# Attention, top-1 experts and a gated product on one core: the first pair's swapped k on TensorE, the last gate's row table inside the written order, own buffers for the last g tile

## The chip, the cores and the metric

The kernel runs on one core of one Trainium2 chip. The metric is the device time of one execution in microseconds (us); lower is better. Before the change the median of three runs is 1043.4 us (1043.09 to 1043.55).

## The reference

Three stages follow each other, all in fp32. The matrix products of the kernel work on pairs of fp32r tiles, a high and a low part of each number, with three products for one.

```python
# attention: 4 batches, 8 heads, 576 positions, 64 wide
scores = q @ k.T / sqrt(64)
scores = where(scores >= rowmax - tau, scores, -1e9)
x = softmax(scores) @ v                       # 2304 tokens x 512
# experts: 8, 1024 wide, the best one for each token
logits = x @ w_gate
g = softmax(logits)[best]
x = g * (relu(x @ w1[best]) @ w2[best])
# gated product, 1536 wide
out = ((x @ w_a) * (x @ w_b)) @ w_out
```

## The kernel before

**Attention** (class `Attention`, lines 257 to 1230). Sixteen pairs of heads are numbered 0 to 15, four for a batch. For a pair, k and q are loaded, split into high and low (`kh`, `kl`, `qh`, `ql`, lines 405 to 437), transposed by TensorE (`qk`, line 460 for four blocks of 128 positions, lines 484 and 485 for the tail of 64 positions) and copied out of PSUM (`qe`). A score product needs k twice, once with its high and low halves swapped between the partitions; the swapped copy `kT[:, 1]` is made by DMA from `kT[:, 0]` (`swap`, line 466; units `sk0` and `sk2`). The nine score tiles of a pair (`s`, line 677; J is the one of the two tails) are followed by the row maximum (`m`, line 690), the threshold (`th`, line 694), the exponential (`e`, line 698) and the masked product (`p`, line 710). The probabilities are transposed (line 785), split (lines 738 to 750) and multiplied with v (line 861, stacked halves `tk` by DMA, line 806), and the result is multiplied with W (line 887), which holds an identity and the gate's columns. The work of several pairs overlaps.

After each batch a **gate** (lines 950 to 1068) takes the expert of each token, counts with small products how many tokens of each expert came before (`tr`), forms the slot of each token (`slot`, lines 1016 to 1027), adds the batch's counts to the running first rows (`base`, line 1037), scales the tokens (`xg0` to `xg3`, `xh`) and scatters them by GpSimd to their expert's rows in DRAM (`sc0` to `sc4`, line 44).

While the last pair runs, a **lead** item already computes 256 rows of one expert from the first three batches (lines 523 to 650): weights are loaded one by one in three raw buffers (`l_wl`, lines 568 and 570), split (`l_wh`, `l_wd`, lines 583 to 589; w1 on ScalarE and VectorE, w2 on GpSimd), and used by eight first products (`l_ap`, line 601; relu `l_ah`, `l_ad`, lines 606 and 610) and eight second ones (`l_b`, line 625).

The order of all this is written out by hand: `ORDER` is a list of some 2750 names, and `emit` calls the units in that order. Each engine executes its own instructions in turn; SyncE's queue does so with the DMAs that it issues.

**Experts** (class `Experts`). `order` (line 1299) sorts the experts by their number of rows and writes a table of the expert, its first rows and count, `ti`. SyncE reads it (line 1605), loads the first expert's rows (`xr`, line 1510), which also need every scatter to have landed, and then the raw weights (line 1440). The rows are transposed (`px`, line 1530), copied and split (lines 1532 and 1533), the weights are split (lines 1446 and 1447), and products follow (lines 1555 and 1576). `order` is no part of the written order; the framework places it between.

**Gated product** (`gated`, line 1711). Seven groups of the 1536 columns go over five chunks of 512 tokens, the last of 256. `front` makes a and b (line 1743), a copy (line 1750), their product (line 1752) and its high and low part `gh`, `gl` (lines 1754 and 1756), in rings of three buffers. `back` makes the output product (line 1769) and adds it to `acc` (line 1774); it is issued one chunk behind `front`. In the last group each finished tile of 128 tokens is scattered to the output (line 44).

```python
    gh, gl = [ap.tile([P, 512], F32R, tag=f"g{r}", bufs=3, name=f"g{r}_{g}_{c0}_{j}") for r in range(2)]
    nc.scalar.copy(gh[:, 0:n], gt[:, 0:n])
    low = nc.vector if (g, c0) == (ng - 1, chunks[-1][0]) else nc.gpsimd
```

## Time and profile before

| | |
|---|---|
| median of three runs | 1043.4 us |
| the profiled execution | 1042.98 us |
| its span, first to last instruction | 1041.3 us |
| TensorE busy in the span | 1003.0 us (96%) |
| VectorE | 713.3 us (68%) |
| ScalarE | 541.7 us (52%) |
| GpSimd | 562.6 us (54%) |

The profile is of one execution. PE is TensorE's products, PEld its weight loads, DVE VectorE, ACT ScalarE, POOL GpSimd, SP SyncE; a q behind an engine's name is its queue, which also issues DMAs. L785 is line 785 of the kernel. A row of the order in time gives the start and the length of a group of like instructions in us, and in brackets how long the engine was idle before it and what ended that. Products are pipelined and their ends are modelled, so that the length of a group is a little more than its number times the distance of two. PEclk is the granted clock of TensorE as a share of full speed (2.4 GHz; half is 1.2 GHz).

### The profile page before, as it was taken

What the parts mean: (1) busy time and instruction counts of PE and PEld (TensorE: products, weight loads), DVE (VectorE), ACT (ScalarE), POOL (GpSimd) and SP (SyncE); (2) the same over time, 40 slices, a digit from 0 to 9 for tenths busy, and PEclk for the clock granted to TensorE, in tenths of its full rate; (3) what the DMA queues carried; (4) which work ended last, traced back from release to release, by engine and by line L of the source; (5) the groups of instructions that cost most, each with busy time, mean ns of one, the idle gap of its engine ahead of it and who ended that gap; (6) DMA issues with size and microseconds to landing.
All of it is one profiled execution on the core that took longest, in us unless ns stands there. A gap on an engine that the chain in (4) does not pass through costs nothing.

```text
span 1041.3 us, 18663 instructions
## 1 busy us (share of the span) xinstructions
PE 1003.0 (96%) x6392; PEld 910.2 (87%) x6392; DVE 713.3 (68%) x1454; ACT 541.7 (52%) x1118; POOL 562.6 (54%) x522
## 2 busy tenths in 40 slices
PE   5899999999999899999999999999999999999996
PEld 4799999999999889999999988888888888888885
DVE  6999999999997545555599488843953945834222
ACT  4999999999996354455565344321322312321110
POOL 4888898998987521111234267633633734623334
PEclk9999999999999989999999999999999999999999
DMA  6778645445344486556666123510210310300012
GB/s 164 216 208 226 183 122 133 110 130 132 104 119 148 163 261 210 168 172 180 191 197 210 34 81 74 68 41 1 63 59 1 81 41 21 82 1 1 31 51 101
DMA packets 111777, 119.20 MB, mean 114 GB/s; under 512 B 20064, under 2 KB 82528, under 8 KB 111680
## 3 DMA queue, kind: packets, MB, share of 16 engines
q1 hardware_dynamic: 107248, 106.93, 37.0%
q0 software_dynamic: 3840, 10.50, 2.7%
q8 instruction: 51, 0.84, 0.3%
q10 hardware_dynamic: 592, 0.56, 0.2%
q14 instruction: 46, 0.38, 0.1%
HBM read 77.57 MB, written 20.98 MB: 95 GB/s over the span
## 4 chain that ended last, share of the span: by engine, by line
PE 52%; issue 5%; POOL 3%; DVE 3%; ACT 1%; POOLq 0%; DVEq 0%; ACTq 0%
PE pg L1743 22%; PE po L1769 10%; PE py_i L1576 9%; PE ph_i L1555 9%; POOL out L44 1%; PE px_i L1530 1%; POOL w L1478 1%; POOL t L1477 1%; DVE acc L1774 1%; DVE a L1469 1%; DVE w L1447 1%; POOL g L1756 0%; DVE t L1473 0%; DVE u L1470 0%; ACT w L1476 0%
## 5 line engine op out<-in xcount | busy, mean ns | idle before, releaser
L1743 PE MATMUL pg<-y,w 128*128 128x512 f32 (+1 forms) x1440 | 301.9, 368 | 0.0
L1743 PEld LDWEIGHTS pg<-y,w 128*128 128x128 f32 x1440 | 251.6, 189 | 45.3
L1756 POOL TENSOR_TENSOR g<-gg,g 128x512 fp32r<-128x512 f32 (+1 forms) x58 | 76.2, 1314 | 151.0 <-ACT g L1754 150.9
L1769 PE MATMUL po<-w,g 128*128 128x512 f32 x648 | 153.3, 390 | 0.6 <-DVE acc L1774 0.6
L1769 PEld LDWEIGHTS po<-w,g 128*128 128x128 f32 x648 | 120.9, 188 | 26.2 <-issue 0.8
L1447 POOL TENSOR_TENSOR w<-raw,w 128x512 fp32r<-128x512 f32 x33 | 45.3, 1373 | 160.5 <-ACT w L1446 154.3
L750 POOL TENSOR_TENSOR pt<-st,pt 128x512 fp32r<-128x512 f32 x93 | 119.8, 1295 | 10.1 <-ACT pt L740 7.2
L1754 ACT CAST g<-gg 128x512 fp32r<-128x512 f32 (+1 forms) x60 | 34.7, 578 | 170.1 <-PE po L1769 97.3
L1555 PE MATMUL ph_i<-xt_i,w 128*128 128x256 f32 (+4 forms) x768 | 118.9, 302 | 4.3 <-DVE w L1447 2.4
L1752 DVE TENSOR_TENSOR gg<-ga,pg 128x512 f32<-128x512 f32 (+1 forms) x60 | 37.7, 629 | 122.0 <-PE pg L1743 122.0
L1576 PE MATMUL py_i<-h_i,w 128*128 128x256 f32 (+4 forms) x768 | 114.0, 297 | 0.3 <-PEq L1670 0.3
L1555 PEld LDWEIGHTS ph_i<-xt_i,w 128*128 128x128 f32 x768 | 106.9, 192 | 6.0 <-DVE w L1447 3.1
L1576 PEld LDWEIGHTS py_i<-h_i,w 128*128 128x128 f32 x768 | 106.5, 192 | 0.7 <-ACT w L1446 0.6
L861 PE MATMUL pv<-pt,sv 128*128 128x288 f32 x512 | 103.3, 317 | 0.2 <-ACT o L866 0.2
L1774 DVE TENSOR_TENSOR acc<-acc,po 128x512 f32<-128x512 f32 x108 | 72.7, 683 | 34.6 <-PE po L1769 34.6
L785 PE MATMUL tp<-idf,P 128*128 128x128 f32 x504 | 89.9, 274 | 2.2 <-DVE P L710 1.3
L1477 POOL TENSOR_TENSOR t<-t,w 128x512 f32<-128x512 f32 x36 | 53.2, 1478 | 64.0 <-ACT w L1476 47.7
L1446 ACT CAST w<-raw 128x512 fp32r<-128x512 f32 x128 | 75.7, 618 | 15.0 <-PE py_i L1576 5.9
L1447 DVE TENSOR_TENSOR w<-raw,w 128x512 fp32r<-128x512 f32 x95 | 68.3, 730 | 11.0 <-ACT w L1446 9.0
L861 PEld LDWEIGHTS pv<-pt,sv 128*128 128x128 f32 x512 | 75.0, 190 | 0.8 <-ACT o L866 0.6
L1560 DVE SCALAR_TENSOR_TENSOR h_i<-ph_i,h_i 128x256 fp32r<-128x256 f32 (+4 forms) x64 | 28.8, 451 | 62.5 <-ACT h_i L1559 62.5
L1559 ACT ACTIVATE h_i<-ph_i 128x256 fp32r<-128x256 f32 (+4 forms) x64 | 26.1, 407 | 83.5 <-PE ph_i L1555 62.7
(249 smaller groups left out, 1920.0 us busy)
## 6 DMA issues: line engine op xcount, KB each, us to landing
raw<-in_moe_w SPq DMA_DIRECT2D x128, 256.0 KB
xs<-zero SPq DMA_DIRECT2D x32, 320.0 KB
tk<-half SPq DMA_DIRECT2D x64, 144.0 KB
raw<-in_moe_w_a SPq DMA_DIRECT2D x12, 512.0 KB
raw<-in_moe_w_b SPq DMA_DIRECT2D x12, 512.0 KB
raw<-in_moe_w_out SPq DMA_DIRECT2D x12, 512.0 KB
kT<-kT SPq DMA_DIRECT2D x32, 160.0 KB
kT<-kT SPq DMA_DIRECT2D x30, 144.0 KB
```

Of the source, the lines that this page charges most:

```text
L750: nc.gpsimd.tensor_sub(lo, st, fr(hi))
L785: nc.tensor.transpose(st["ps"][:, 128 * j:128 * j + 128], parts(j), idf)
L861: nc.tensor.matmul(R["v", n][:, 0:HALF], lhs, z, start=(c == 0 and r == 0), stop=(c == 4))
L1446: nc.scalar.copy(hi_t, raw)
L1447: engine.tensor_sub(lo_t, raw, fr(hi_t))
L1477: g.tensor_sub(t, t, fr(hi))
L1555: nc.tensor.matmul(ps[:, 0:n], w[a][:, k, :], xt[b][k][:, 0:n], start=(s_ == 0), stop=(s_ == len(steps) - 1))
L1576: nc.tensor.matmul(st["y"][d][:, 0:n], w[a][:, 0, d * P:d * P + P], h[b][:, 0:n], start=(f == 0 and d % each == 0 and (a, b) == (0, 0)), s ...
L1743: mm = nc.tensor.matmul(ps[:, 0:n], w[g][j][m][a][:, k, :], self.y[b][:, k, c0:c0 + n], start=(s_ == 0), stop=(s_ == len(steps) - 1))
L1756: last = low.tensor_sub(gl[:, 0:n], gt[:, 0:n], fr(gh)[:, 0:n])
L1769: nc.tensor.matmul(ps, res[j][a][:, t * P:t * P + P], w[g][j][2][b][:, 0, :], start=(s_ == 0), stop=(s_ == len(steps) - 1))
L1774: nc.vector.tensor_tensor(acc[:, tt, :], acc[:, tt, :], ps, op=ALU.add)
```

## The change

- Pair 0: GpSimd splits the tails of k and q (units `kH`, `qH`, `kL`, `qL`), a second copy of k's high part is laid behind the low part (`k3` on ScalarE, `K3` for the tail on GpSimd), and TensorE transposes low and high in that order (`sk0`, `sk2`, and a third block of the tail). ScalarE and VectorE copy the results to `kT[:, 1]`. The four swap DMAs of this pair are gone. The tails' loads are split in two DMAs of 64 rows each, k's on SyncE's and q's on ScalarE's queue; tau goes to SyncE's queue. In the order the constants (`c:r`, `c:m`) come first, the tail's transposes before all others, and the zero fills of `qj` and `z` go from VectorE to GpSimd.
- Last gate: `order` is gone. Its instructions are in the last gate's `base`, in two new units `places` and `table`, and three of them in the lead's selection; most operands lie in the PSUM bank of the gate's counts. The integer table comes straight from a sum, no longer from a copy. In the new order the five last scatters stand in a row behind `table`.
- Gated product: in the last chunk of the last group the second `gh`, `gl` get the buffers of two tiles of the weight splits (`mag`, `t`), and the last tile's output product and sum are done in two halves of 256 columns.
- `ORDER` is new throughout.

```diff
 ORDER = """
-qh:0 qH:0 kh:0 kl:0 qk:0:k2 qk:0:k0 kH:0 qe:0:k2 kL:0 ql:0 qL:0 c:z qk:0:t qe:0:k0 qe:0:kt qk:0:q0 qk:0:q1 c:t qe:0:q1
-qe:0:q0 qe:0:sk0 qe:0:t qe:0:sk2 s:0 qh:1 c:r ql:1 kh:1 kl:1 z:10 z:17 vh:0 vl:0 lv:1 vh:1 vl:1 c:w s:1 qk:1:t qe:1:t
+c:r c:m kh:0 qh:0 k3:0 kl:0 kH:0 qH:0 kL:0 qL:0 K3:0 qk:0:t qk:0:k0 qe:0:ks qe:0:k0 qk:0:k2 c:z qk:0:sk0 qk:0:sk2 ql:0
+c:t qe:0:k2 qk:0:q0 qk:0:q1 qe:0:sk2 qe:0:q1 qe:0:t qe:0:sk0 qe:0:kt lk:2 kh:1 kl:1 vh:0 vl:0 qh:1 ql:1 qe:0:q0 s:0
...
+s:1 m:0 m:1 e:0 th:1 p:0 e:1 qk:1:t qe:1:t qk:1:k0 qk:1:q0 qe:1:q0 qe:1:k0 qe:1:kt s:2 p:1 s:3 m:2 m:3 th:3 e:2 p:2
...
+l_wh:4:0 l_wd:4:0 l_wl:4:1 l_b:0 x1s:15 x1t:15 lt:gate:15 tl:gate:15 L:gate:15 top:gate:15 shift:gate:15 ex:gate:15
+g:gate:15 l_ap:2 l_ah:2 l_ad:2 l_b:1 tr:gate:15 l_hint slot:gate:15 base:gate:15 l_wh:4:1 l_wd:4:1 l_wl:5:0 l_wh:5:0
+xg0:gate:15 l_wd:5:0 l_wl:5:1 l_wh:5:1 l_wd:5:1 xg3:gate:15 l_ap:3 l_ah:3 l_ad:3 places:gate:15 l_b:2 xg1:gate:15
+xg2:gate:15 l_ap:4 l_ah:4 xh:gate:15 table:gate:15 l_ad:4 l_b:3 l_ap:5 sc0:gate:15 sc1:gate:15 sc2:gate:15 sc3:gate:15
+sc4:gate:15 gate:15 l_wl:6:0 l_wh:6:0 l_wd:6:0 l_wl:6:1 l_wh:6:1 l_wd:6:1 l_wl:7:0 l_wh:7:0 l_ah:5 l_wd:7:0 l_wl:7:1
...
         for n in "kq":
-            nc.sync.dma_start(self.state[0]["raw_" + n][:, 8, :], two[n][:, 512:576].rearrange("a s d -> a s d"))
+            for a in range(2):
+                (nc.sync if n == "k" else nc.scalar).dma_start(self.state[0]["raw_" + n][64 * a:64 * a + 64, 8, :], two[n][a, 512:576])
...
             for z in self.qj:
-                nc.vector.memset(fr(z), 0.0)
-            nc.vector.memset(self.z, 0.0)
+                nc.gpsimd.memset(fr(z), 0.0)
+            nc.gpsimd.memset(self.z, 0.0)
...
+        def again(z):
+            def run():
+                o, x = s["sk"][:, z, 2, :], s["raw_k"][:, z]
+                if z == tail:
+                    nc.gpsimd.tensor_scalar(o, x, 1.0, 1.0, op0=ALU.mult, op1=ALU.mult)
+                else:
+                    nc.scalar.copy(o, x)
+            return run
...
+        def again(n):
+            def front():
+                if "S" not in ps:
+                    ps["S"] = self.psS.tile([P, 2, 512], F32R, tag="S", name="again")
+                for j in range(4):
+                    nc.tensor.transpose(ps["S"][:, n, P * j:P * j + P], kb(4 * n + j, 1), idr)
+
+            def back():
+                (nc.vector.tensor_copy if n else nc.scalar.copy)(tile("kT")[:, 1, 640 * n:640 * n + 512], flat(ps["S"])[:, n])
+            return front, back
...
             pre = G["pre"]
-            if b == self.B - 2:
+            if last:
+                counts[:] = cnt, key, G2 = bank(112, E), bank(120, E), bank(128, E * E)
+                v.tensor_tensor(cnt, pre[:, 5], r["rest"], op=ALU.add)
+                v.scalar_tensor_tensor(key, cnt, float(E), r["io"], op0=ALU.mult, op1=ALU.subtract)
+                same = new("key", [P, E])
+                v.tensor_copy(same, key)
+                v.tensor_copy(r["src"][:, 2, :], cnt)
+                v.tensor_tensor(grid(G2), key.unsqueeze(1).to_broadcast([P, E, E]), same.unsqueeze(2).to_broadcast([P, E, E]), op=ALU.is_gt)
+            elif b == self.B - 2:
...
+        def table():
+            big = bank(256, 4 * E * E).rearrange("p (z a b) -> p z a b", z=4, a=E)
+            shape = [P, 4, E, E]
+            v.tensor_tensor(big, grid(bank(192, E * E)).unsqueeze(1).to_broadcast(shape), r["src"].unsqueeze(2).to_broadcast(shape), op=ALU.mult)
+            with nc.allow_low_precision(reason="one whole number and zeros"):
+                v.tensor_reduce(r["ti"], big, axis=AX.X, op=ALU.add)
+            v.tensor_reduce(r["T"], big, axis=AX.X, op=ALU.add)
+            v.tensor_copy(r["st"], bank(48, E))
+            self.psT.done(G["pr"])
...
-                    gh, gl = [ap.tile([P, 512], F32R, tag=f"g{r}", bufs=3, name=f"g{r}_{g}_{c0}_{j}") for r in range(2)]
+                    end = (g, c0) == (ng - 1, chunks[-1][0])
+                    if end and j:
+                        gh, gl = [self.cv.tile([P, 512], F32R, tag=z, name=f"g_{z}") for z in ("mag", "t")]
+                    else:
+                        gh, gl = [ap.tile([P, 512], F32R, tag=f"g{r}", bufs=3, name=f"g{r}_{g}_{c0}_{j}") for r in range(2)]
...
+                    wide = DM // 2 if (g, tt) == (ng - 1, ntile - 1) else DM
+                    for z in range(0, DM, wide):
+                        z = slice(z, z + wide)
```

## Rows read from the trace of the kernel before

**Rows 1.** Busy time by stage: length, then engines (instructions), PEclk, DMA share, GB/s.
```profile
0.00:16.00 16.00, 5.13 (x26) 4.41 (x27) 10.16 (x41) 4.83 (x10) 7.36 (x25) 1.00 0.64 161
...
100.00:200.00 100.00, 98.17 (x785) 92.74 (x785) 92.34 (x239) 94.68 (x203) 89.85 (x92) 1.00 0.55 149
...
337.00:360.00 23.00, 21.00 (x175) 20.32 (x174) 14.78 (x49) 6.94 (x15) 14.25 (x14) 1.00 0.40 135
360.00:374.00 14.00, 9.45 (x40) 8.91 (x41) 5.91 (x11) 6.83 (x14) 4.85 (x5) 0.63 0.72 241
374.00:1017.00 643.00, 639.84 (x3581) 566.28 (x3580) 381.35 (x604) 223.94 (x449) 247.91 (x190) 1.00 0.32 91
```

**Rows 2.** Waits of TensorE, 60 to 345 us: us in all, times, longest.
```profile
PE pv L861 <- DMA tk<-half: 1.3, 2, 0.6
```

**Rows 3.** Instructions in order of time, start of the kernel.
```profile
4.81 1.26 PE L460 MATMUL tq<-idr,sk 128*128 128x128 f32 x8 [4.81 <-DVE sk L428]
...
6.86 0.24 ACT L419 CAST sq<-raw_q 128x64 fp32r<-128x64 f32 x1 [1.90 <-DMA raw_q<-in_q]
7.01 0.58 ACT L476 CAST kT<-tq 128x512 fp32r<-128x512 f32 x1
...
14.48 1.81 PE L677 MATMUL S_J<-kT,qj 128*128 128x288 f32 x6 [3.99 <-DMA kT<-kT]
```

**Rows 4.** GpSimd's groups up to 345 us: count, busy us, mean ns of one.
```profile
L827 POOL TENSOR_TENSOR pt<-js,pt 128x256 fp32r<-128x256 f32 x32 | 23.8, 748 | 7.9 <-ACT pt L826 7.8
...
L589 POOL TENSOR_TENSOR l_w<-l_raw,l_w 128x512 fp32r<-128x512 f32 x5 | 7.0, 1402 | 0.3
L717 POOL TENSOR_SCALAR J<-J 128x64 f32<-128x64 f32 x16 | 4.0, 250 | 0.3 <-DVE J L710 0.2
...
L585 POOL TENSOR_SCALAR l_w<-l_raw 128x512 fp32r<-128x512 f32 x5 | 3.1, 621 | 4.2 <-DMA l_raw<-in_moe_w 4.2
```

**Rows 5.** VectorE in order of time, 343 to 358 us.
```profile
343.64 0.22 DVE L1027 TENSOR_SCALAR si<-slot,role 128x1 int32<-128x1 f32 x1
...
349.32 0.42 DVE L610 SCALAR_TENSOR_TENSOR l_h<-l_ph,l_h 128x256 fp32r<-128x256 f32 x1 [2.20 <-ACT l_h L606]
...
352.81 0.69 DVE L589 TENSOR_TENSOR l_w<-l_raw,l_w 128x512 fp32r<-128x512 f32 x1 [2.09 <-ACT l_w L583]
...
355.40 0.80 DVE L1327 TENSOR_TENSOR o_big<-o_M,src 128x256 f32<-128x256 f32 x1
...
356.69 0.70 DVE L1331 CAST o_ti<-o_T 128x32 int32<-128x32 f32 x1
```

**Rows 6.** The other engines in order of time, 351 to 373 us.
```profile
351.82 0.99 POOL L44 DMA_INDIRECT xs<-xg,si  x1 [0.30 <-issue]
...
354.70 1.69 PE L601 MATMUL l_ph<-l_xT,l_w 128*128 128x256 f32 x12 [1.52 <-DVE l_h L610]
...
358.53 0.37 SPq L1510 DMA_DIRECT2D xr_i<-xs  x1
...
362.49 2.58 PE L1530 MATMUL px_i<-idf,xr_i 128*128 128x128 f32 x12 [2.56 <-DMA xr_i<-xs]
...
366.83 6.23 PE L1555 MATMUL ph_i<-xt_i,w 128*128 128x352 f32 x24 [1.76 <-ACT w L1446]
```

**Rows 7.** Instructions in order of time, the tail.
```profile
1018.25 5.92 PE L1743 MATMUL pg<-y,w 128*128 128x256 f32 x48
...
1024.00 8.35 PE L1769 MATMUL po<-w,g 128*128 128x512 f32 x36
...
1028.76 0.41 ACT L1754 CAST g<-gg 128x256 fp32r<-128x256 f32 x1 [5.57 <-PE po L1769]
1029.20 0.42 DVE L1756 TENSOR_TENSOR g<-gg,g 128x256 fp32r<-128x256 f32 x1 [0.21 <-ACT g L1754]
...
1032.16 1.28 DVE L1774 TENSOR_TENSOR acc<-acc,po 128x512 f32<-128x512 f32 x2 [1.80 <-PE po L1769]
...
1034.41 0.98 POOL L44 DMA_INDIRECT out<-acc,i_idc  x1 [0.30 <-issue]
```

More of the change, by code (lines that the diff above doesn't have):

```diff
@@ L342, in rest, with more @@
                 )
+        def more():
+            i2, ji = tiles["i2"], tiles["ji"]
+            routing.update(routing.pop("late")())
             nc.vector.tensor_copy(self.II, i2.unsqueeze(1).to_broadcast([P, 2, D]))
@@ L365, in wide @@
             nc.vector.tensor_copy(self.WT[:, :, W:WT], self.W2[:, 4:8, D:W])
-        self.setup = {"t": scales, "z": zeros, "r": rest, "w": wide}
+        self.setup = {"t": scales, "z": zeros, "r": rest, "w": wide, "m": more}
     def load(self, i, names):
@@ L426, in run @@
                 t = s["s" + n][:, z]
-                g = nc.vector if n != "v" and (i, n) in self.FIRST else nc.gpsimd
+                g = nc.vector if n != "v" and (i, n) in self.FIRST and not (i == 0 and z == tail) else nc.gpsimd
                 g.tensor_sub(t[:, :, 1, :], s["raw_" + n][:, z], fr(t)[:, :, 0, :])
@@ L482, in tails, with again_tail @@
         def tails():
-            t = ps["t"] = self.psT.take(F32R, f"tt{i}", 2)
+            t = ps["t"] = self.psT.take(F32R, f"tt{i}", 2 + (i == 0))
             nc.tensor.transpose(t[:, 0:P], qb(8), idr)
             nc.tensor.transpose(t[:, P:2 * P], kb(8), idr)
+            if i == 0:
+                nc.tensor.transpose(t[:, 2 * P:3 * P], kb(8, 1), idr)
+        def again(n):
[7 more added lines that the diff above has]
+            return front, back
+        def again_tail():
+            t = fr(ps["t"])
+            nc.scalar.copy(tile("kT")[:, 1, 512:640], t[:, 2 * P:3 * P])
+            nc.scalar.copy(tile("kT")[:, 1, 1152:1216], t[:, 2 * P + 64:3 * P])
+            self.psT.done(ps["t"])
         def tails_evac():
@@ L520, in lead_select @@
         v.tensor_scalar(r["kept"], top[:, 0:1], float(LEAD), float(LEAD), op0=ALU.is_ge, op1=ALU.mult)
+        v.tensor_scalar(cnt, r["sel"], r["kept"], None, op0=ALU.mult)
+        v.tensor_tensor(r["src"][:, 3, :], cnt, r["eb"], op=ALU.add)
+        v.tensor_tensor(r["rest"], ps[:, 112:112 + E], r["src"][:, 3, :], op=ALU.subtract)
         self.psT.done(ps)
@@ L1038, in bases, with places @@
                 self.psT.done(G["pr"])
+        grid = lambda z: z.rearrange("p (a b) -> p a b", a=E)
+        if last:
+            bank = lambda lo, m: G["pr"][:, lo:lo + m]
+            counts = [None] * 3
+        def places():
+            cnt, key, G2, rk, M, st = *counts, bank(104, E), bank(192, E * E), bank(48, E)
+            row, col = lambda z: z.unsqueeze(1).to_broadcast([P, E, E]), lambda z: z.unsqueeze(2).to_broadcast([P, E, E])
+            v.tensor_reduce(rk, grid(G2), axis=AX.X, op=ALU.add)
+            v.tensor_tensor(grid(G2), grid(G2), row(r["src"][:, 2, :]), op=ALU.mult)
+            v.tensor_tensor(grid(M), row(rk), col(r["io"]), op=ALU.is_equal)
+            v.tensor_reduce(st, grid(G2), axis=AX.X, op=ALU.add)
+            v.tensor_scalar(r["src"][:, 1, :], st, r["kept"], None, op0=ALU.add)
+        def table():
[7 more added lines that the diff above has]
+            self.psT.done(G["pr"])
         def scaled(t):
@@ L1065, in gate @@
         return [("lt", tail), ("tl", sum_tail), ("L", logits), ("top", top), ("shift", shifted), ("ex", exps),
-                ("tr", ranks), ("g", weight), ("slot", slots), ("base", bases), *[(f"xg{t}", scaled(t)) for t in range(4)], ("xh", scaled_tail),
+                ("tr", ranks), ("g", weight), ("slot", slots), ("base", bases), *((("places", places), ("table", table)) if last else ()), *[(f"xg{t}", scaled(t)) for t in range(4)], ("xh", scaled_tail),
                 *[(f"sc{t}", rows(t)) for t in range(5)]]
@@ L1166, in run @@
                             **{f"xg{t}": ["g"] for t in range(4)}, **{f"sc{t}": [f"xg{t}", "slot"] for t in range(4)}, sc4=["xh", "slot"])
+                if i == n - 1:
+                    need.update(base=["tr"], places=["base"], table=["places", "slot"])
                 for k, f in self.gate(i // 4):
@@ L1813, in attention_experts_gated @@
         sel=c.tile([P, E], F32, name="sel"),
+        rest=c.tile([P, E], F32, name="rest"),
+        st=c.tile([P, E], F32, name="st"),
+        T=c.tile([P, 4, E], F32, name="T"),
+        ti=c.tile([P, 4, E], I32, name="ti"),
         kept=c.tile([P, 1], F32, name="kept"),
```

408 lines of the change are left out of this document (189 added, 219 removed).

## The prediction, made before the changed kernel ran

> **What bounds the kernel now.** I read first the busy time by stage [rows 1]. From 374 us to 1017 us TensorE is busy for 639.8 of 643.0 us at full clock, and in the attention it is busy 98.2 of every 100. A microsecond gained early therefore reaches the end, because what follows is TensorE work back to back; its longest wait in the attention is 1.3 us in all, for a stacked half by DMA [rows 2]. TensorE stands idle in three places, and the change touches just these: the start (5.1 us busy of 16.0), the end of the attention with the hand-over to the experts (337 to 374 us: 2.0 + 4.55 us idle, and the granted clock falls to a mean of 0.63 of full in the second part), and the tail after 1017 us. Then I read each place in order of time: the start [rows 3], the prices of small GpSimd work [rows 4], VectorE before the hand-over [rows 5], what that stretch holds up [rows 6], and the tail [rows 7].
>
> In the start the reader is to see one wait: TensorE begins the first score product and then stands still for 3.99 us until a DMA has brought the swapped halves of k (14.48 us). In the hand-over it is a chain: the slots are ready at 343.86 us (343.64 + 0.22), but the table that is built behind them ends only at 357.39 us (356.69 + 0.70), because VectorE, which works in order, waits 2.20 us for the lead item's relu and 2.09 us for a weight in between. SyncE reads the table, issues the rows of the first expert at 358.53 us, TensorE waits 2.56 us for them and after that 1.76 us for the split of the first weight.
>
> The sum is made against the profiled execution: 1042.98 us, of which the span is 1041.3 us. That execution lies 0.4 us below the median of the runs, 1043.4 us, and I do not correct for it. A measurement of this kernel can tell about 0.2%, 2.1 us, from no change.
>
> **Part 1, the start.** Removed: four swap DMAs, two on SyncE's and two on ScalarE's queue, and the wait for them. Added on TensorE: nine transposes (27 instead of 18); 8 of them take 1.26 us [rows 3], so 0.16 us each and 4.3 us for all 27. All of them now stand behind the tails, whose split goes to GpSimd: a copy each for q, k and the second k, 0.25 us each [rows 4], and two subtractions of 64 elements, between 0.25 (a copy of that size) and 0.75 us (a subtraction of 256); I take 0.4, nearer to the copy, as the size is the same. Before, the q tail was taken up at 6.86 us. If it lands then, what is left (copy, two subtractions, copy) takes 0.25 + 0.4 + 0.4 + 0.25 = 1.3 us and TensorE starts at 8.2 us. The q tails now go out on ScalarE's queue ahead of its table load instead of last on SyncE's, so they can land up to a microsecond earlier, 7.2 us. I take 7.6 us. The transposes end at 7.6 + 4.3 = 11.9 us. ScalarE copies in between: the second k's 512 columns 0.58 us [rows 3], the first k's, and the tails; the second bank goes to VectorE. They end before 11.9 us. The eight score matmuls then start at once: six took 1.81 us, so 2.4 us, up to 14.3 us instead of 14.48 + 1.81 = 16.29 us. **Gain 2.0 us.** Bounds: 1.4 us with the late tail; nothing if the ramp after it does not pass it on; the most is 3.7 us, if the tails come early and the eight run at the pace of the attention.
>
> Edits that I cost at nothing: the constants moved to the front (some fifteen small VectorE instructions, two w_gate DMAs on SyncE behind the loads, where the swaps stood) lie in the time before k lands; the memsets moved to GpSimd lie behind K3 and ahead of the first use of qj, about 2 us later; if that cover is short, each of the three costs between a small and a 512-element copy, 0.25 to 0.62 us, on the path of qj alone. The three instructions added to the lead's selection fall where VectorE is busy 92.3 us of 100. The rest of the written-out order is new as well. Each engine executes it in turn, so it can win or lose small waits anywhere in the attention; TensorE has only 1.8 us per 100 to win, and I put it at 0, with 3 us on either side.
>
> **Part 2, the hand-over.** The order of the experts becomes part of the written-out order and its operands lie in PSUM. Behind the slots stand five small instructions (0.2 us each), one weight split (0.7 us), a relu subtraction (0.42 us, 349.32 [rows 5]), five more, and the table (two to four instructions of 0.2 to 0.8 us). From 343.86 us that is 1.0 + 0.7 + 0.4 + 1.0 + 0.9 = 4.0 us without waits, 348 us; with two waits like those of before it is 352 us. SyncE reads it about 1.1 us later (357.39 to 358.53 us), so in both cases before the rows of the experts are written.
>
> What is late next is GpSimd: split of weight 5, the scaled tile, five scatters in a row at 1.28 us (0.99 us for the last one, at 351.82 us, and the 0.30 us that stand between two [rows 6, 7]), then the splits of weights 6 and 7 that TensorE needs for its last two products. A split is a copy of 0.62 and a subtraction of 1.40 us, the tile like the copy [rows 4]. I put the start at 342 us, a little ahead of the slots: 2.0 + 0.6 + 5 x 1.28 = 9.0 us, so the scatters end at 351.0 us and two more splits at 355.0 us. If GpSimd starts only with the slots, all this is 1.9 us later. The scatters' landing is not shown. It takes at least nothing and at most 358.53 - 352.81 = 5.7 us, since the rows were then issued without a wait for them; I take 2 us, nearer to nothing, because reading 704 KB back took 3.96 us and a scatter moves a fraction of it. The rows go out at 353 us and land 362.49 - 358.53 = 3.96 us later, at 357 us. TensorE's lead work ended at 362.49 - 2.56 = 359.93 us with 2.0 us of stalls [rows 1], mainly the 1.52 us at 354.70 [rows 6], which went back to the 2.09 us wait for a weight whose load was issued late. Now loads 5 and 6 are released before the scatters, the stalls go, and TensorE ends at 357.9 us. The rows are there.
>
> So 2.0 us of stalls and 2.56 us of waiting fall away. The twelve transposes that took 2.58 us under the fallen clock take 12 x 0.16 = 1.9 us, 0.7 us less. The 1.76 us for the first weight stays. **Gain 5.2 us.** Bounds: nothing, if the rows land as late as before; 7.4 us if the clock is also held over that last wait.
>
> **Part 3, the tail.** With buffers of its own the last g tile no longer waits for a product of the chunk before (5.57 us at 1028.76 [rows 7]). TensorE did not stand still: 36 products in 8.35 us, 0.232 us apart, without a gap. But their order did change: both last tiles end together, their sums are two in a row at 1032.16 us, and their scatters go out at 1033.13 and 1034.41 us. With the tile ready, tile 16 ends with the 30th product, 1024.00 + 30 x 0.232 = 1030.96 us, and its scatter starts 0.97 us later as before (1032.16 to 1033.13), at 1031.93 us. Tile 17 is now 12 half products at 5.92/48 = 0.123 us, up to 1032.44 us, its last half sum takes 0.42 us as the 256-column row at 1029.20 does, and its scatter follows at 1033.2 us, behind the first one (0.98 + 0.30 us). That is 1.2 us before 1034.41 us; I take **1.1 us**, between nothing and 1.2.
>
> **Sum:** 2.0 + 5.2 + 1.1 = 8.3 us, 1042.98 - 8.3 = **1034.7 us**. Its own range, with the order at 3 us to either side and the tail as it is, is 1031.5 to 1037.5 us.
>
> **Rivals.**
> *The clock is kept.* The six score matmuls took 0.3 us each where the attention needs 0.125 (98.17 us for 785), after TensorE had stood idle [rows 3]; if the unbroken transposes ahead of them bring it up to full pace, the eight take 1.0 us, 1.4 us less. And the 24 first products (6.23 us) ran at a granted clock of half; if the clock is held they could take 3.1 us less, of which I count 2, since the second product's weights come next. That gives 1034.7 - 3.4 = 1031.3 us. Against it: the 1.76 us wait stays, and one of that length stands beside the low clock. The Trainium skill (TensorE: Matmul & The Clock Gate, What's actually happening) says that the throttled state is the default and that sustained work releases it. By that rule the denser start would be the 1.4 us faster; the trace agrees in pace, but its clock column shows 1.00 there. Chance 0.14.
> *A new wait in place of the table's.* The scatters now all stand behind one another and ahead of the splits of weights 6 and 7. If GpSimd starts them 3 us later than I think, the splits end at 358 us, TensorE waits before its last two products and then for the rows. The part brings 1.5 instead of 5.2 us: 1038.4 us. For it: the last scatter started at 351.82 us before, with these two splits still behind it. Chance 0.20.
> *The order costs more than it brings.* ScalarE is busy 94.7 us of 100 in the attention. If the new order makes ScalarE wait more in each of the 16 head pairs, it takes the place of TensorE as the bound. At 0.4 us a pair this is 6.4 us, 1041.1 us, within 0.2%; from 0.65 us a pair (2.1 + 8.3 = 10.4 us) it decides the sign, and at 0.8 us the time is 1047.5 us. Against it: ScalarE gets new work in the first pair only. Chance 0.06 for no change and 0.06 for slower.
> *The change does not do what it says:* the swapped k waits for the tails as long as it did for the DMA (from a GpSimd end at 10 us on). The start brings nothing, 1036.7 us; this lies in the range of the forecast.
>
> **The numbers.** The forecast has 0.54, with the start's failure in it. Faster: 0.54 + 0.14 + 0.20 = 0.88; within 0.2%: 0.06; slower: 0.06. The range takes in the clock's rival below (1031.3, less a little for the order) and the new wait above (1038.4, and 1.6 us for the order): 1030.4 to 1040.0 us. Outside are the two cases of the order and the edges of the others, a little under 2 in 10.
>
> **What would show it.** In the changed profile the first score product starts near 12 us without a wait for kT by DMA; the integer table is written near 348 to 352 us, the first rows are issued near 353 us, and the lead's last product is followed at once by the transposes of the rows, at a full granted clock; the first products of expert 0 start 7 us earlier than 366.83. In the tail the last two scatters start near 1.1 us earlier against the end of the products, the sums no longer two in a row. It is wrong if SyncE's wait before the rows ends on a scatter after 357 us, if TensorE waits for a GpSimd split of weight 6 or 7, or if TensorE's idle time in the attention grows by several (100 to 200 us: 1.8 us now).

## The result and the profile after

The changed kernel takes 1029.69 us (median of four runs, 1027.01 to 1031.18), the kernel before 1043.47 us in the same runs: a ratio of 0.9864, 95% interval 0.9842 to 0.9886. That is 13.8 us gained where 8.3 were forecast, and 0.7 us below the lower end of the range. Four later runs of the same kernel (`after_again`, below) gave 1031.19 us, a ratio of 0.9889 (0.9872 to 0.9905); that median lies inside the range, 1030.4 to 1040.0 us. The runs of the changed kernel spread over 4 us, and the profiled one is the fastest of its four, 1027.01 us (span 1025.3 us); both have to be kept in mind when its rows are read.

Busy time by stage of the changed kernel, with the columns of [rows 1]:

```profile
0.00:16.00 16.00, 7.62 (x55) 6.88 (x56) 11.77 (x42) 8.72 (x20) 10.65 (x33) 1.00 0.52 136
...
100.00:200.00 100.00, 99.17 (x804) 94.58 (x803) 94.46 (x252) 96.89 (x211) 92.53 (x94) 1.00 0.55 150
...
337.00:360.00 23.00, 21.63 (x168) 20.81 (x167) 13.25 (x36) 10.60 (x24) 12.76 (x14) 1.00 0.69 217
360.00:374.00 14.00, 14.00 (x86) 13.29 (x86) 7.26 (x16) 6.86 (x14) 3.21 (x4) 1.00 0.98 301
```

TensorE's idle time in the hand-over falls from 2.0 + 4.55 us to 1.4 us, all of it before 360 us, and the granted clock no longer falls from 360 to 374 us (1.00, 0.63 before).

The start, in order of time (GpSimd and TensorE); it answers to [rows 3]:

```profile
5.06 0.24 POOL L433 TENSOR_SCALAR sk<-raw_k 128x64 fp32r<-128x64 f32 x1 [1.06 <-DMA raw_q<-in_q]
...
6.66 0.37 PE L503 MATMUL tt<-idr,sq 128*128 128x128 f32 x1 [6.66 <-DVE tau_abs L328]
...
10.12 0.40 PE L720 MATMUL S_J<-kT,qj 128*128 128x288 f32 x1
...
10.88 1.19 PE L720 MATMUL S_J<-kT,qj 128*128 128x288 f32 x7 [0.36 <-ACT kT L533]
```

GpSimd takes up the tails at 5.06 us, the transposes begin at 6.66 us, the first scores at 10.12 us and end at 12.07 us instead of 16.29 us. Seven score products take 1.19 us, where six took 1.81 us. The clock column reads 1.00 for the first 16 us of both kernels, so the start is judged by the pace of the products.

The hand-over, all engines in order of time; it answers to [rows 5, 6]. The last two lines are SyncE's waits before it issues the rows (us in all, times, longest):

```profile
336.65 0.21 DVE L1070 TENSOR_SCALAR si<-slot,role 128x1 int32<-128x1 f32 x1
...
340.35 0.42 DVE L1110 TENSOR_REDUCE ti<-tr 128x32 int32<-128x256 f32 x1
...
342.94 0.98 POOL L44 DMA_INDIRECT xs<-xh,si  x1 [0.30 <-issue]
...
346.03 1.70 PE L644 MATMUL l_ph<-l_xT,l_w 128*128 128x256 f32 x12 [1.07 <-DVE l_h L653]
...
346.29 0.37 SPq L1555 DMA_DIRECT2D xr_i<-xs  x1
...
351.90 1.38 PE L1575 MATMUL px_i<-idf,xr_i 128*128 128x128 f32 x12
352.52 1.52 ACT L1577 CAST xt_i<-px_i 128x352 fp32r<-128x352 f32 x4 [1.48 <-PE px_i L1575]
...
353.06 1.67 PE L668 MATMUL l_py<-l_h,l_w 128*128 128x256 f32 x12
353.90 1.17 ACT L1491 CAST w<-raw 128x512 fp32r<-128x512 f32 x2
...
354.60 4.36 PE L1600 MATMUL ph_i<-xt_i,w 128*128 128x352 f32 x24
...
359.26 2.81 PE L1621 MATMUL py_i<-h_i,w 128*128 128x352 f32 x16 [0.30 <-PEq L1715]
...
SPq L1555 <- DMA xs<-xg,si: 1.1, 1, 1.1
SPq L1555 <- DMA xs<-xh,si: 0.8, 1, 0.8
```

The reader is to see two things. The slots are ready at 336.86 us, the table at 340.77 us, and the rows of the first expert go out at 346.29 us, held by the landing of the scatters (GpSimd ends the last at 343.92 us) and not by the table. And the transposes of the rows (`px_i`) stand ahead of the lead's last product (`l_py` at 353.06 us), not behind it. While that product runs, ScalarE and VectorE copy the rows and ScalarE makes the first weight's high part, so the first products follow at 354.60 us without any wait, at full clock: 24 in 4.36 us, not 6.23. Most of the 1.4 us that TensorE is idle is the lead's wait at 346.03 us for VectorE's part of a relu.

The tail; it answers to [rows 7]:

```profile
1015.60 1.13 DVE L1826 TENSOR_TENSOR acc<-acc,po 128x512 f32<-128x512 f32 x2 [0.67 <-PE po L1821]
...
1016.78 0.62 PE L1821 MATMUL po<-w,g 128*128 128x256 f32 x3 [0.51 <-DVE acc L1826]
...
1017.80 0.42 DVE L1826 TENSOR_TENSOR acc<-acc,po 128x256 f32<-128x256 f32 x1 [1.07 <-PE po L1821]
1018.49 0.98 POOL L44 DMA_INDIRECT out<-acc,i_idc  x1 [0.95 <-DVE acc L1826]
```

TensorE waits 0.51 us ahead of the second half of the last tile, until VectorE has summed the first: both halves lie in one tile of PSUM, the only thing that the two instructions share.

**Five stretches.** To compare many executions I cut each at the same five rows of the timeline: A up to the third group of twelve of the lead's first products (`l_ph`, behind most of the attention), B from there to the first group of second products of expert 0 (`py_i`, 373.36 us before, 359.26 after), C to the twelve first products that wait 0.46 to 0.49 us for a weight's low part, D to VectorE's last multiplication of the gated product (`gg`), E to the start of the last scatter. In the kernel before they are:

```profile
328.01 1.70 PE L601 MATMUL l_ph<-l_xT,l_w 128*128 128x256 f32 x12
...
373.36 0.89 PE L1576 MATMUL py_i<-h_i,w 128*128 128x352 f32 x4 [0.30 <-PEq L1670]
...
540.56 1.69 PE L1555 MATMUL ph_i<-xt_i,w 128*128 128x256 f32 x12 [0.46 <-DVE w L1447]
...
1024.30 0.42 DVE L1752 TENSOR_TENSOR gg<-ga,pg 128x256 f32<-128x256 f32 x1 [1.56 <-PE pg L1743]
```

| profiled execution | A | B | C | D | E |
|---|---|---|---|---|---|
| before | 328.01 | 45.35 | 167.20 | 483.74 | 10.11 |
| after | 322.57 | 36.69 | 167.36 | 482.25 | 9.62 |
| after_again | 323.20 | 36.84 | 168.82 | 482.26 | 9.63 |
| no_halves | 323.18 | 36.86 | 168.76 | 483.76 | 9.05 |
| early | 323.65 | 36.04 | C + D: 650.27 | | 9.05 |
| table_late | 323.71 | 42.26 | 167.13 | 482.29 | 9.62 |
| px_behind | 324.00 | 40.23 | 167.14 | 483.80 | 9.63 |
| swap_back | 330.64 | 36.44 | 169.08 | 482.27 | 9.63 |
| start_only | 324.70 | 46.26 | 167.22 | 482.26 | 10.11 |
| tail_own | 326.65 | 44.89 | 167.23 | 483.77 | 9.05 |
| tail_both | 328.41 | 45.74 | 168.30 | 483.81 | 9.62 |
| fill_hand | 326.89 | 44.19 | 167.83 | 482.25 | 10.12 |
| fill_start | 327.17 | 46.85 | 167.32 | 483.76 | 10.11 |

Between the two profiled executions: A -5.4, B -8.7, C +0.2, D -1.5, E -0.5, together -15.9 of the 16.0 us between them. D is no effect of the change: it has two values, 482.3 and 483.8, in old and new kernels alike (below). In `after_again` the same sum is -4.8 - 8.5 + 1.6 - 1.5 - 0.5 = -13.7.

### The profile page after: what moved, and what is told of

It is laid out like the page before. It is cut to its first block, busy times and chain, and to the rows that moved or that the text cites. A ratio compares the mean times of both kernels' runs of the same rounds, so it can differ in the third digit from the quotient of the medians.

```text
span 1025.3 us, 18703 instructions
## 1 busy us (share of the span) xinstructions
PE 996.6 (97%) x6407; PEld 904.3 (88%) x6407; DVE 712.7 (70%) x1453; ACT 541.3 (53%) x1121; POOL 563.9 (55%) x530
## 4 chain that ended last, share of the span: by engine, by line
PE 52%; issue 5%; POOL 3%; DVE 3%; ACT 1%; POOLq 0%; DVEq 0%; ACTq 0%
PE pg L1788 22%; PE po L1821 11%; PE py_i L1621 9%; PE ph_i L1600 9%; POOL out L44 1%; PE px_i L1575 1%; POOL w L1523 1%; POOL t L1522 1%; DVE acc L1826 1%; DVE w L1492 1%; DVE a L1514 1%; POOL g L1805 0%; DVE t L1518 0%; DVE u L1515 0%; ACT w L1521 0%
## 5 line engine op out<-in xcount | busy, mean ns | idle before, releaser
L1600 PE MATMUL ph_i<-xt_i,w 128*128 128x256 f32 (+4 forms) x768 | 116.7, 298 | 2.5 <-DVE w L1492 2.4
L1600 PEld LDWEIGHTS ph_i<-xt_i,w 128*128 128x128 f32 x768 | 104.7, 189 | 4.4 <-DVE w L1492 3.3
L1826 DVE TENSOR_TENSOR acc<-acc,po 128x512 f32<-128x512 f32 (+1 forms) x109 | 73.0, 679 | 34.3 <-PE po L1821 34.3
L1795 ACT COPY ga<-pg 128x512 f32<-128x512 f32 (+1 forms) x60 | 32.6, 543 | 68.6 <-PE pg L1788 68.6
```

The lines of the kernel that those rows point to most:

```text
L1600: nc.tensor.matmul(ps[:, 0:n], w[a][:, k, :], xt[b][k][:, 0:n], start=(s_ == 0), stop=(s_ == len(steps) - 1))
L1826: nc.vector.tensor_tensor(acc[:, tt, z], acc[:, tt, z], ps[:, z], op=ALU.add)
```

## The experiments

All were compared with the kernel before on the same chip. The first four take the change apart.

**tail_own**, the kernel before with only the buffers of its own for the last g tile:

```diff
+                    end = (g, c0) == (ng - 1, chunks[-1][0])
+                    if end and j:
+                        gh, gl = [self.cv.tile([P, 512], F32R, tag=z, name=f"g_{z}") for z in ("mag", "t")]
```

> The kernel before with the last g tile's own buffers alone, no halves. If the gain of the tail comes from the two last tiles no longer ending together: 0.9 to 1.2 us faster than before, the two last sums apart and the last scatter about 1 us earlier against the start of the last chunk. If the tail is set by something else (the scatters' queue, the last landing): no change.

Measured: 1042.32 us, ratio 0.9989 (0.9979 to 1.0000), 1.1 us below the kernel before. Its last rows:

```profile
1030.63 0.69 DVE L1781 TENSOR_TENSOR acc<-acc,po 128x512 f32<-128x512 f32 x1 [0.67 <-PE po L1776]
1031.59 0.98 POOL L44 DMA_INDIRECT out<-acc,i_idc  x1 [0.38 <-DVE acc L1781]
```

E is 9.05 us, 1.06 us less: the sums are no longer two in a row. That is the buffers' whole worth.

**tail_both**, the same with the two halves of the last tile:

```diff
+                    wide = DM // 2 if (g, tt) == (ng - 1, ntile - 1) else DM
```

> The kernel before with the whole third part, own buffers and the last tile in halves. By the step of the prediction: 1.1 us faster, as much as with own buffers alone or a little more. By the rival from the changed profile: the second half waits for the sum of the first half (0.51 us there), so it is only about 0.5 us faster, 0.4 to 0.7 us slower than with own buffers alone.

Measured: 1043.22 us, ratio 0.9996 (0.9985 to 1.0007). E is 9.62 us: the halves give back 0.57 us, by the same 0.51 us wait as in the changed kernel. The times are too close for more than a hint; the rows decide.

**start_only**, the kernel before with the code of the new start and the head of the new order:

```diff
-qh:0 qH:0 kh:0 kl:0 qk:0:k2 qk:0:k0 kH:0 qe:0:k2 kL:0 ql:0 qL:0 c:z qk:0:t qe:0:k0 qe:0:kt qk:0:q0 qk:0:q1 c:t qe:0:q1
+c:r c:m kh:0 qh:0 k3:0 kl:0 kH:0 qH:0 kL:0 qL:0 K3:0 qk:0:t qk:0:k0 qe:0:ks qe:0:k0 qk:0:k2 c:z qk:0:sk0 qk:0:sk2 ql:0
...
```

> The kernel before with the first part alone: its code and the new order up to the first score tile, then the old order. If the start is worth the 4.2 us that the first score tile ends earlier in the changed profile: 3.5 to 4.5 us faster. If the prediction's 2.0 us was right and the rest came from the new order of the attention: 1.5 to 2.5 us. If the ramp does not pass it on: under 1 us.

Measured: 1039.70 us, ratio 0.9963 (0.9949 to 0.9977), 3.7 us below the kernel before. TensorE:

```profile
11.08 2.05 PE L716 MATMUL S_J<-kT,qj 128*128 128x288 f32 x7 [0.19 <-ACT kT L532]
...
28.87 2.56 PE L716 MATMUL S_J<-kT,qj 128*128 128x288 f32 x8
```

Here the seven products ran at the half pace; they end at 13.13 us, 3.2 us earlier than before. Then the granted clock, once up, fell again (0.57 from 24 to 32 us), and the second pair's eight J products took 2.56 us. Even so A is 3.3 us shorter. The hand-over is the old one (B 46.26, 0.9 us longer).

**swap_back**, the changed kernel with the first pair's swap by DMA again (its units right behind the copies of k, all else new):

```diff
-            u["sk0"], u["sk2"] = again(0), again(1)
+            u["sk0"], u["sk2"] = ((lambda: None), lambda: swap(0, 640)), ((lambda: None), lambda: swap(640, 1216))
```

> The changed kernel with the first pair's swapped k made by DMA again, in the new order. If the start is the transposes in place of the DMA: 3 to 4.5 us slower than the changed kernel (1033 to 1034), the first score tile ends at 16 us again. If the tails' early split and the constants at the front do it: under 1.5 us slower.

Measured: 1037.58 us, ratio 0.9943 (0.9920 to 0.9966).

```profile
14.26 1.78 PE L718 MATMUL S_J<-kT,qj 128*128 128x288 f32 x6 [2.90 <-DMA kT<-kT]
...
362.38 4.34 PE L1598 MATMUL ph_i<-xt_i,w 128*128 128x352 f32 x24
```

This is 7.9 us above the changed kernel's 1029.69 us, where 3 to 4.5 were expected. The wait for the swap is back, and A becomes 330.64, longer than before by 2.6 us. The start does not explain that: from the end of the first J scores (16.04 us) to the end of A this execution takes 314.6 us, all the others 310.2 to 311.7. So with the swap by DMA the new order loses some 3 to 4 us later in the attention. Two waits for a stacked half by DMA (`tk`), 1.1 us between 60 and 92 us, which the changed kernel has not, are part of it; the rest was not found. B is 36.44: the hand-over needs nothing of the start.

The next four ask what each stretch is made of.

**table_late**, the changed kernel with the table and the loads that read it behind the lead's relu subtraction of unit 5:

```diff
-xg2:gate:15 l_ap:4 l_ah:4 xh:gate:15 table:gate:15 l_ad:4 l_b:3 l_ap:5 sc0:gate:15 sc1:gate:15 sc2:gate:15 sc3:gate:15
+xg2:gate:15 l_ap:4 l_ah:4 xh:gate:15 l_ad:4 l_b:3 l_ap:5 sc0:gate:15 sc1:gate:15 sc2:gate:15 sc3:gate:15
...
+l_ad:5 places:gate:15 table:gate:15 gate:15 l_b:4
```

> The changed kernel with only the hand-over's list put back late: the scatters stay where they are, but the places, the table of the experts and the loads that read it stand behind the lead's relu subtraction of unit 5, so the table is ready near 350 us instead of 340.8 us. In the changed kernel the rows are issued at 346.29 us, behind the scatters, and the transposes of the rows (351.90 us) come before the lead's last product. Theory that the earlier table is what the hand-over gained: the rows go out 5 to 6 us later, near 352 us, land near 356 us, TensorE waits before the last product or the transposes by 1 to 3 us, the granted clock falls in the wait, and the time is 3 to 6 us above the changed kernel's 1029.7 us, near 1034. Theory that the hand-over was bound by TensorE's own list (the lead's stalls) and not by the table: no wait for the rows, at most 1 us more, near 1030.

Measured: 1035.63 us, ratio 0.9917 (0.9902 to 0.9932).

```profile
347.33 0.42 DVE L1110 TENSOR_REDUCE ti<-tr 128x32 int32<-128x256 f32 x1
...
352.66 1.06 PE L1575 MATMUL px_i<-idf,xr_i 128*128 128x128 f32 x8 [0.59 <-DMA xr_i<-xs]
...
355.11 1.07 ACT L679 CAST l_y<-l_py 128x512 fp32r<-128x512 f32 x2 [4.18 <-PE px_i L1575]
...
356.44 1.52 ACT L1577 CAST xt_i<-px_i 128x352 fp32r<-128x352 f32 x4 [0.25 <-ACT l_y L679]
...
358.52 1.54 PE L1600 MATMUL ph_i<-xt_i,w 128*128 128x352 f32 x4 [3.15 <-ACT w L1491]
```

The table is 7.0 us later, but the rows only 2.45 us (issued at 348.74 us), since the scatters held them before; in both, 1.1 us is this execution's longer A. That is enough: part of the transposes falls behind the lead's last product, ScalarE's copies of the lead's output go ahead of those of the rows, the first products wait 3.15 us, and the clock falls (24 in 6.9 us with a gap). B is 5.6 us longer than in the changed kernel.

**fill_hand**, the kernel before with idle transposes in the two waits of the hand-over:

```diff
+            for _ in range(21):
+                nc.tensor.transpose(st["ph"][:, 0, 0:P], self.consts["idf"], self.consts["idf"])
...
                for f in prep[0][1]:
                    f()
+                d = self.psy.tile([P, 512], F32, tag="y0", name="fill_y")
+                for _ in range(14):
+                    nc.tensor.transpose(d[:, 0:P], self.idf, self.idf)
```

> The kernel before with 21 transposes that nothing reads between the lead's last product and the transposes of the rows, and 14 more behind those, so that TensorE works through both of its waits (2.56 and 1.76 us); nothing else changes. Theory that the clock is a term of its own here: the 12 transposes take 1.4 instead of 2.58 us and the 24 first products 4.4 instead of 6.23 us with the waits as they were, together 3.0 us, so 2 to 3 us below the kernel before, near 1040.8. Theory that only the order of the work counts (the wait for the weights' split sets the start of the first products and the weights that come next set their pace): the granted clock rises, but the time stays within 0.7 us of the kernel before.

Measured: 1042.78 us, ratio 0.9989 (0.9980 to 0.9998).

```profile
362.03 1.40 PE L1536 MATMUL px_i<-idf,xr_i 128*128 128x128 f32 x12 [0.37 <-DMA xr_i<-xs]
...
365.20 4.34 PE L1561 MATMUL ph_i<-xt_i,w 128*128 128x352 f32 x24 [0.24 <-ACT w L1452]
...
371.08 0.92 PE L1582 MATMUL py_i<-h_i,w 128*128 128x352 f32 x4 [1.54 <-ACT h_i L1565]
```

The clock is held and the two groups take what was expected, 3.1 us less. Half of it comes back at once: the next product waits 1.54 us for ScalarE's relu, which stands behind a weight's copy that begins at 369.75 us, hardly earlier than the 370.08 us of the kernel before. With the rows late, the clock alone is worth about 1 us (1.0 in the median, 1.2 in B), between what the two theories expected.

**fill_start**, the kernel before with idle transposes in the wait for the swapped half:

```diff
+                    if (i, kind, j) == (0, "J", 0):
+                        d = self.psV.tile([P, 512], F32R, tag="V", name="fill")
+                        for _ in range(26):
+                            nc.tensor.transpose(d[:, 0:P], self.consts["idr"], self.consts["idr"])
```

> The kernel before with 26 transposes that nothing reads after the first two products of the first pair's S_J, so that TensorE works through most of its 3.99 us wait for the swapped half; nothing else changes. Theory that the start's gain is partly the clock: the six products after the wait take 1.0 to 1.2 instead of 1.81 us, the A products behind them 0.79 instead of 1.16 us, and the eight A products of 19.51 us 1.5 instead of 2.26 us; VectorE's first J pass starts about 0.7 us earlier and the time falls by 1 to 2 us, near 1042. Theory that the start's gain is only the missing wait: the six products start at 14.5 us as before and the end moves by less than 0.5 us, since the ramp waits for VectorE's passes.

Measured: 1042.47 us, ratio 0.9984 (0.9975 to 0.9993).

```profile
14.74 1.06 PE L678 MATMUL S_J<-kT,qj 128*128 128x288 f32 x6 [1.41 <-DMA kT<-kT]
...
22.24 1.30 PE L678 MATMUL S_A<-kT,qT 128*128 128x288 f32 x4 [0.88 <-DVE P L715]
...
31.67 1.30 PE L678 MATMUL S_J<-kT,qj 128*128 128x288 f32 x8
```

The clock rises: six products in 1.06 us. But in this execution, the slowest of the eleven (1043.79 us), it fell again in the ramp (0.74 and 0.62 in the two stretches from 16 to 32 us), and the second pair begins at 31.67 us, in the kernel before at 31.70 us. In the median 1.3 us remain.

**no_halves**, the changed kernel with the last tile in one piece:

```diff
-                    wide = DM // 2 if (g, tt) == (ng - 1, ntile - 1) else DM
+                    wide = DM
```

> The changed kernel with the very last tile of the output in one piece again: 6 half-size products become 3 pairs of full ones, 12 products of 512 columns over, one sum and one scatter; the buffers of its own stay. In the changed kernel the second half's first product waits 0.51 us for the sum of the first half, as both lie in one tile of PSUM; from the last gate multiplication to the last scatter it is 9.62 us there (1008.87 to 1018.49) and 10.11 us before. Theory that the halves cost: 9.05 us, the last scatter starts 0.57 us earlier, and the time is about 0.6 us below the changed kernel's. Theory of the prediction, that the halves bring the smaller last sum: the distance grows to 9.9 us or more.

Measured: 1030.11 us, ratio 0.9859 (0.9844 to 0.9874). The last tile's twelve half-size products are six full ones here. E is 9.05 us, 0.57 less than in the changed kernel, to the digit as expected. In the time this does not show, as the runs differ by more.

The last three go after the order in the hand-over and the spread.

**px_behind**, the changed kernel with the rows' transposes ordered behind the lead's last product, as they were before:

```diff
-                        nc.tensor.matmul(ps, w[a][:, d * P:d * P + P], h[b],
+                        self.routing["lead_relu"][2] = nc.tensor.matmul(ps, w[a][:, d * P:d * P + P], h[b],
...
-                                         start=(f == 0 and d % 2 == 0 and (a, b) == (0, 0)), stop=(f == F - 1 and d % 2 == 1 and a == 1))
+                                         start=(f == 0 and d % 2 == 0 and (a, b) == (0, 0)), stop=(f == F - 1 and d % 2 == 1 and a == 1)).ins
```

> The changed kernel with one thing put back in TensorE's order: the twelve transposes of the first expert's rows stand behind the lead's last product, as in the kernel before, instead of ahead of it (the copies of the lead's output then also go out on ScalarE ahead of the rows' copies, as before); table, scatters and row loads stay early. Theory that the transposes ahead of the last product hide the wait for the first weight's split and so hold the clock: the rows are there, the transposes start near 353.3 us without a wait for a DMA, but the first products wait 1.8 to 3.2 us for ScalarE and VectorE and run partly at the half clock (5 to 6.2 instead of 4.36 us); the time is 2 to 5 us above the changed kernel's, near 1033. Theory that the early rows alone are the gain: the first products wait less than 0.5 us, the time is within 1 us of the changed kernel's.

Measured: 1034.22 us, ratio 0.9915 (0.9899 to 0.9932). TensorE:

```profile
353.51 1.38 PE L1575 MATMUL px_i<-idf,xr_i 128*128 128x128 f32 x12
357.16 1.11 PE L1600 MATMUL ph_i<-xt_i,w 128*128 128x352 f32 x4 [2.27 <-ACT w L1491]
358.92 4.94 PE L1600 MATMUL ph_i<-xt_i,w 128*128 128x352 f32 x20 [0.66 <-DVE w L1492]
```

The rows are there, yet the first products wait 2.27 and 0.66 us and then run partly at the half clock (granted 0.50 from 359 to 361 us). B is 40.23, 3.5 us longer than in the changed kernel and 5.1 us shorter than before: the early table, scatters and rows with the old order of the end bring 5.1 of the 8.7 us, the new order the other 3.5. As ScalarE's copies of the lead's output go first again too, the 3.5 us belong to both orders, TensorE's and ScalarE's, together.

**after_again**, the changed kernel once more, no edit:

> The changed kernel once more, in more runs, as the base for the kernel below and to see what the runs near 1030 to 1031 us have that the one of 1027 us had not. Theory that it is the clock behind the 1.93 us wait for a weight's low half near 554 us, and a wait of about 1 us for the second pair of weights of the first expert near 366 us: a median of 1029 to 1030.5 us, and if the profiled run is above 1029 us one or both of these stand in its trace. Theory that the runs differ in the attention: the lead's third product starts 2 us or more later than 322.57 us and the later stages are the same.

Measured: 1031.19 us (1029.27 to 1033.05), ratio 0.9889. The profiled run, 1029.27 us, differs from that of 1027.01 us in C: TensorE waits 1.01 us at 366.57 us for ScalarE's split of a weight, and ScalarE for its load. The DMA share, 0.96 from 360 to 374 us, does not explain it: it is 0.98 in the execution without the wait. The same wait stands in `no_halves` (0.93) and `early` (0.86). The row:

```profile
366.57 2.60 PE L1600 MATMUL ph_i<-xt_i,w 128*128 128x352 f32 x12 [1.01 <-ACT w L1491]
```

The clock behind the 1.91 us wait was kept here, so this execution shows only one of the two causes, and the median lies above the 1029 to 1030.5 us expected; what the slowest runs have was not profiled.

**early**, `no_halves` with the early gate-weight splits spread over other experts:

```diff
-    EARLY = ((2, 4), (2, 6), (1, 0), (1, 4), (1, 6), (0, 0))
+    EARLY = ((3, 2), (3, 6), (2, 2), (2, 6), (1, 2), (1, 6))
```

> The changed kernel without the halves of the last tile, and with the six early splits of the first gate weights handed out two for each of the fifth, sixth and seventh expert, none for the last, instead of two, three and one for the sixth, seventh and eighth; VectorE is busy 10.6 of 20 us in the experts before them and nearly without a break where TensorE waits 0.47 and 1.93 us. Theory that VectorE's crowding is that wait: it shrinks or goes, the clock is held behind it in each run, and the time is 1.5 to 3.5 us below the changed kernel's (0.6 of it from the tail), near 1027.5. Theory that the wait comes from the loads or from the order and not from the gate weights: it moves and the time stays within 1 us of the changed kernel's.

Measured: 1028.08 us (1027.68 to 1029.90), ratio 0.9859 (0.9842 to 0.9875). TensorE's waits there:

```profile
548.78 1.45 PE L1600 MATMUL ph_i<-xt_i,w 128*128 128x256 f32 x10 [0.27 <-DVE w L1492]
...
552.34 1.45 PE L1600 MATMUL ph_i<-xt_i,w 128*128 128x256 f32 x10 [0.44 <-DVE w L1492]
...
554.49 0.50 PE L1600 MATMUL ph_i<-xt_i,w 128*128 128x256 f32 x2 [0.69 <-ACT w L1491]
...
555.40 1.45 PE L1600 MATMUL ph_i<-xt_i,w 128*128 128x256 f32 x10 [0.41 <-DVE w L1492]
```

The wait of 0.46 us is gone, the one of 1.92 us has become four short ones with nearly the same sum (1.81 us), and the clock stays up. So the crowding by the gate weights sets the place of the wait, but not most of its size. Of the kernels run it has the lowest median: 3.1 us below `after_again`, 1.6 us below the changed kernel's first four runs. But its ratio to the kernel before is that of `no_halves`, and C + D, 650.27, lies between the changed kernel's own two executions (649.61 and 651.08). That the spread splits shorten the time is not shown, and one execution with the clock kept does not show that they keep it in each run.

## Why the prediction was right and wrong

**The chain of the hand-over held, the step that ended it did not.** From the slots to the table 4.0 us were forecast without waits, and 340.77 - 336.86 = 3.91 us were measured; from the slots to the end of the scatters 351.0 - 343.86 = 7.1 forecast, 343.92 - 336.86 = 7.06 measured; from there to the issue of the rows 2 and 2.4 us. All of it lies 7.0 us earlier than forecast, as the slots do (336.86 and not 343.86 us); 5.4 us of that is stretch A. That the wait before the rows would end on the scatters and no longer on the table was right too. What failed is the sentence "The 1.76 us for the first weight stays." It took TensorE's order from the kernel before, the lead's last product and behind it the transposes. With the rows early, the framework, which places these instructions outside the written order, put the transposes first (in `table_late`, with the rows 2.45 us later, eight ahead of the lead's last eleven products and four behind); the last product then covers the copies and the split. The forecast 5.2 us is what `px_behind`, which has the assumed order, gives: B falls by 45.35 - 40.23 = 5.1 us. Part of that agreement is luck, as its waits before the first products are 2.93 us and not 1.76, while the transposes save 1.2 us and not 0.7. That its time, 1034.22 us, is near the forecast 1034.7 us is luck too: its start gains more than 2.0 us and its tail less than 1.1. The changed kernel has 8.7 us: 3.5 us more, which is the waits (2.93 us) and the clock (24 products in 1.11 + 4.94 = 6.05 us and not 4.36), less the 1.07 us of the lead's wait at 346.03 us, a stall that by the forecast was to go and that `px_behind` has not.

**The clock.** The rival "The clock is kept" named 2 us at the first products; 6.23 - 4.36 = 1.9 us were measured. The runs bear it out, but as a consequence: where a wait stays before the first products they run partly or wholly at the half clock (6.23 us before, granted 0.50 from 367 to 371 us; 4.94 for 20 in `px_behind`; 5.38 for 20 in `table_late`, granted 0.50 from 358 to 364 us), and where it goes they take 4.36. For the other half of that rival, 1.4 us at the start, the runs say "sometimes": the seven products took 1.19 us in `after`, `no_halves` and `px_behind`, 1.94 to 2.05 us in `after_again`, `early`, `table_late` and `start_only`. It is also smaller than named: the eight products take 12.07 - 10.12 = 1.95 us in `after` and 2.70 us in `after_again`, 0.75 us apart. The Trainium skill (TensorE: Matmul & The Clock Gate, What's actually happening), cited in the forecast for its rule that activity releases the throttle, says further that the moment varies from run to run; these rows agree.

**The start was mis-sized: 2.0 forecast, 3.2 to 4.2 at the end of the first J scores.** Three terms were off. The tails were taken up at 5.06 us, where the forecast had 5.9 to 6.9 us, so TensorE began at 6.66 instead of 7.6 us: 0.9 us. The 27 transposes took 3.5 instead of 4.3 us (10.12 - 6.66): 0.8 us; the price of 0.16 us each came from the modelled length of a group of eight, 1.26 us, while the next group starts 1.01 us after it (7.08 and 8.09 us in the changed kernel). And in some executions the clock was already up: the eight scores took 1.95 instead of 2.4 us. The bound of 3.7 us was set for early tails at full pace and was still too small by 0.5 us. Stretch A fell by 4.0 to 5.4 us in the kernels with the new start and order; executions with the old start differ by 1.8 us among themselves (326.65 to 328.41, the kernel before near the upper end), so this part is known to about 1 us only. That the new order brings nothing to the attention by itself, as forecast, is supported: from the end of the first J scores to the end of A the six executions with the new start and order take 310.2 to 311.7 us, the five with the old start 310.3 to 311.7 us, and `start_only` with the old order 311.6 us.

**The tail was over-sized: 1.1 forecast, 0.5 measured.** The buffers bring 1.06 us; the halves, counted as a gain, cost 0.57 us, because the second one waits for VectorE on the same tile of PSUM, a wait of 0.51 us that the forecast did not see. The Trainium skill (PSUM — Partial Sum Buffer, PSUM bank collisions raise a hardware error) says that the hardware does not hold two engines apart that work in one bank at once, but reports an error, so that a program has to keep them apart itself; the row's wait agrees with that, and no run here shows the error.

**The signs and the rivals.** Faster was right. So was the first score product without a wait for kT by DMA, at 10.12 and not near 12 us. The lead's last product followed at once by the transposes did not come, as told above; the first products of expert 0 start 12.2 us earlier and not 7. The new wait in place of the table's did not come: GpSimd began the scatters at 337.50 us, 0.6 us after the slots, and no wait of TensorE in the hand-over names a GpSimd split. ScalarE did not become the bound: TensorE is busy 99.17 us of 100.

**What stays open:** why in C 1.4 to 1.5 us come and go between executions of the new code with an equal B (a wait for a weight's load accounts for 0.9 to 1.0 of it, and why that load is late is not known), and what the slowest runs of the changed kernel have. The mean granted clock does not order them: 0.998 in the run of 1027.01 us, 0.997 in that of 1031.18 us, 0.993 in that of 1030.30 us.

## What to carry to other kernels

When a load comes earlier, ask what its consumer can now be placed ahead of: here the new order at the end, one TensorE group covering the copies that the other needs, was worth 3.5 us on top of the 5.1 us that the early table and rows brought with the old one. A wait in front of a long group costs twice if the clock falls in it, but paying for the clock alone with idle transposes brought only a third, as the next operand was late anyway. And two halves of one sum that share a tile of PSUM cost time here; whether they gain with a tile for each was not tried.

## What was not expected of the hardware

The same wait, 1.91 to 1.93 us for a weight's low part near the end of the experts, costs the clock in some executions and not in others, in old and new kernels alike. In `no_halves` and in the changed kernel:

```profile
556.46 2.45 PE L1600 MATMUL ph_i<-xt_i,w 128*128 128x256 f32 x10 [1.91 <-DVE w L1492]
```

```profile
554.32 1.45 PE L1600 MATMUL ph_i<-xt_i,w 128*128 128x256 f32 x10 [1.93 <-DVE w L1492]
```

Stretch D, which is the same code in eleven of the kernels, takes 483.74 to 483.81 us in six of the twelve executions and 482.25 to 482.29 us in the other six, and nothing between. In the first six the granted clock is 0.72 over some 6 us around this wait, in the others 1.00: 1.5 us, like the toss of a coin. No one kernel was profiled with both values, so that one and the same kernel tosses anew in each run is not shown, nor is what decides it. In the pair of profiled executions it fell for the changed kernel, so 1.5 of the 16.0 us between them are not the change's. And a clock that is brought up early may fall again in a ramp with waits of about a microsecond (`fill_start`, `start_only`, and `px_behind`, whose start is the changed kernel's: granted 0.57 to 0.74 in stretches of 8 us between 16 and 32 us), while in the first profiled execution of the changed kernel it stayed (1.00) through three waits of 1.2 to 1.3 us at the same place.
